# Four blocks in one first layer: a mixture of experts behind block attention on one core

## Chip, core and metric

The kernel runs on one core of a Trainium2 chip. The metric is device time in microseconds (us) of one launch, as the median of three runs.

## What is computed

The first part is a local-and-summary attention over 4 batches, 8 heads, 768 positions and 64 dimensions. Its output, 3072 rows of 512 numbers, is the input of the second part, a mixture of eight experts in which every row goes to one expert:

```python
logits = np.einsum('bsd,de->bse', x, w_gate)
local_gate = 1.0 / (1.0 + np.exp(-np.einsum('bsd,de->bse', x, w_local).squeeze(-1)))
...
            fresh_e = int(np.argmax(logits[b, s]))
            if s == 0 or local_gate[b, s] < 0.5:
                e = fresh_e
            else:
                e = prev_e if prev_e >= 0 else fresh_e
            prev_e = e
            ...
            h = np.maximum(x[b, s] @ w1[e], 0.0)
            out[b, s] = p[e] * (h @ w2[e])
```

All of it is fp32. The big products are made of three fp32r products each: both factors are split into a high and a low part, and high x high, high x low and low x high are added in PSUM.

## The kernel before, in words

**Attention** (lines 157 to 490) fills the first 120 us or so. While it runs, the rows of the first batch are routed, and the expert that most of them go to is chosen. Its two matrices are loaded and split, and blocks of 128 rows of that expert can start before the routing of the rest is known.

**Blocks and slots.** The rows of an expert are gathered in blocks of 128 by an indirect DMA on GpSimd (`gather`, L1027) into one of two buffers `xg`. `tx` (L1041) transposes a block on TensorE (four transposes, L1038) into a PSUM bank; ScalarE casts it to the high part (L1031) and VectorE subtracts for the low part (L1033), both into `xT`. `pair` (L1138) works on two blocks: its first layer has 8 slices of 128 hidden units, each 4 contraction steps of three matmuls with 256 columns (L1149 to L1151); every two slices share a PSUM bank, which ScalarE takes through ReLU (L1155) and VectorE finishes with the low part (L1157). Its second layer has for each block 8 steps of three matmuls with 512 columns (`mm`, L1055 to L1057), then `store` scales the rows and scatters them (L1081). `single` does one block.

**Order of the work.** All engines run their instructions in the order in which the program writes them. Blocks 0 to 5 are the early ones (`EARLY = 6`): three pairs of the first expert, whose instructions are interleaved with the steps of the routing by a small planner (`flow`, L543), which keeps estimated times of VectorE and TensorE and issues the next step of a chain (`self.steps`) when it thinks that it can run. `finish` is the chain of the second routing: some 65 small VectorE operations (L795 to L974) lead to a table of words, which two matmuls bring into one row (L978); the words say which expert each slot belongs to, and start the load of the next expert's two matrices into `stg`. Then 24 matmuls (L908) give the gather indices of blocks 6 and up, and after a softmax three products `bp` (L995) and 24 matmuls (L999) give `psort`, the rows' gate values.

**Placed steps.** During the second layer of a pair, at the step numbers in `PM`, `PM0`, `PW1` and `PW2`, the blocks of the next pair are transposed, and the matrices of the next expert are split, quarter by quarter: ScalarE casts 1024 columns (L1013), then VectorE (L1016) or GpSimd (L1021, four pieces) subtracts. A quarter of the second matrix can be cast only when the last block has used it. When a matrix is split, the load of a later one is started (`refill`). Blocks 6 to 13 are four sure pairs, with the steps of two experts that have fewer than 32 rows left (`few`) between; from 14 on a slot is a pair or a single by a test at run time. In this run two slots are singles, one of them the last.

Of the kernel before, what the change touches and what calls it, by code (L numbers as in the profile page):

```python
# [19 lines left out]
P = 128  # L20
NP = H // 2
# [26 lines left out]
FEW_AT = 34  # L48
# [16 lines left out]
PM, PM0 = (2, 5), (10, 13)  # L65
# [12 lines left out]
class Kernel:  # L78
# [962 lines left out]
    def tx(self, i, half=0, bank="t"):  # L1041

        ps = self.transposes(lambda c: self.xg[i % 2][:, c, G9:G9 + P], bank).rearrange("p (k t) -> p k t", k=KT)
        self.split_ps(ps, self.xT[:, :, 0, half], self.xT[:, :, 1, half])

    def th(self, src, name):
        ps = self.transposes(lambda c: src[:, P * c:P * c + P], "t")
        h, l = [self.fw.tile([P, 512], F32R, name=name + x) for x in "hl"]
        self.split_ps(ps, h, l)
        return h, l  # L1050
# [8 lines left out]
    def store(self, yp, i, act=False, alone=False):  # L1059
        while self.have_p <= i:  # L1060
            self.small(1, True)
        if i >= LATE and (i % 2 or alone):
# [3 lines left out]
        y = self.mw2.tile([P, 512], F32, name="yo", bufs=2)  # L1066
# [17 lines left out]
    def few_rows(self, j):  # L1084

        t = self.xm[j]
        self.nc.gpsimd.indirect_dma_start(out=t.rearrange("p a d -> p (a d)"), out_offset=None, in_=self.x_rows,
                                          in_offset=bass.IndirectOffsetOnAxis(ap=self.gidx[0:FEW, SLOTS + j:SLOTS + j + 1], axis=0))

    def few_prep(self, j):  # L1090

        nc, fw, b = self.nc, self.fw, j
        i = SLOTS + j
        ps = self.bank("t")
        for c in range(KT):
            nc.tensor.transpose(out=ps[:, FEW * c:FEW * c + FEW], in_=self.xm[b][:, c, G9:G9 + P], identity=self.ident[0:FEW, 0:FEW])
        nc.vector.tensor_copy(out=self.xf[b].rearrange("p k t -> p (k t)"), in_=ps[:, 0:KT * FEW])
        rp = fw.tile([FEW, 2], F32, name="rp")
        nc.vector.tensor_copy(out=rp[:, 0:1], in_=self.sidx[0:FEW, i:i + 1])
        nc.vector.tensor_copy(out=rp[:, 1:2], in_=self.psort[0:FEW, i:i + 1])  # L1100
        yield
        ps = self.bank("t")
        nc.tensor.matmul(out=ps[:, 0:2], lhsT=self.four, rhs=rp, start=True, stop=True)
        nc.vector.tensor_scalar(out=self.idx4[b], in0=ps[:, 0:1], scalar1=4.0, scalar2=self.c["quad"], op0=ALU.mult, op1=ALU.add)
        nc.vector.tensor_copy(out=self.p4[b], in_=ps[:, 1:2])

    def few(self, j):
# [12 lines left out]
        ps = self.bank("t")[:, 0:DF // 4]  # L1120
        for c in range(2):
            nc.tensor.transpose(out=ps[:, P * c:P * c + P], in_=h[:, P * c:P * c + P], identity=self.ident)
        hT = fw.tile([P, 2, 4, FEW], F32, name="fhT")
        nc.vector.tensor_copy(out=hT.rearrange("p c q t -> p (c q t)"), in_=ps)
        yield
        ps = self.bank("a")[:, 0:P]
        for f in range(FT):
            for q in range(4):
                c0 = f * DM + P * q
                nc.tensor.matmul(out=ps[FEW * q:FEW * q + FEW], lhsT=hT[:, f % 2, f // 2], rhs=s2[:, c0:c0 + P],  # L1130
                                 start=(f == 0), stop=(f == FT - 1))
        y = fw.tile([P, P], F32, name="fy")
        nc.vector.tensor_scalar(out=y, in0=ps, scalar1=self.p4[b], scalar2=None, op0=ALU.mult)
        nc.gpsimd.indirect_dma_start(out=self.out.rearrange("t (q d) -> (t q) d", q=4),
                                     out_offset=bass.IndirectOffsetOnAxis(ap=self.idx4[b], axis=0),
                                     in_=y, in_offset=None, bounds_check=4 * T_ALL - 1, oob_is_err=False)

    def pair(self, i, mid, w1, w2):  # L1138

        nc = self.nc  # L1140
        xT, hT = self.xT, self.hT
        for f in range(0, FT, 2):
            ps = self.bank("s").rearrange("p (f t) -> p f t", f=2)
            for j in range(2):
                for k in range(KT):
                    c0 = 2 * P * (KT * (f // 2) + k) + P * j
                    xh, xl = [xT[:, k, part].rearrange("p h t -> p (h t)") for part in range(2)]
                    wh, wl = [w[0][:, c0:c0 + P] for w in (self.hi, self.lo)]
                    nc.tensor.matmul(out=ps[:, j], lhsT=wh, rhs=xh, start=(k == 0), stop=False)  # L1149
                    nc.tensor.matmul(out=ps[:, j], lhsT=wh, rhs=xl, start=False, stop=False)  # L1150
                    nc.tensor.matmul(out=ps[:, j], lhsT=wl, rhs=xh, start=False, stop=(k == KT - 1))  # L1151
                    if k % 2:
                        yield
            h, l = hT[:, f:f + 2, 0], hT[:, f:f + 2, 1]
            nc.scalar.activation(out=h, in_=ps, func=AF.Relu)  # L1155
            self.dve(0.6, self.t + 0.5)
            nc.vector.scalar_tensor_tensor(out=l, in0=ps, scalar=0.0, in1=h.bitcast(F32), op0=ALU.max, op1=ALU.subtract)  # L1157
        for half in range(2):
            yp = self.ya if half and 2 * i >= LATE else self.bank("a")
            s = slice(P * half, P * half + P)  # L1160
            for f in range(FT):
                self.mm(yp, hT[:, f, 0, s], hT[:, f, 1, s], 1, lambda t: t[:, f * DM:f * DM + DM], f == 0, f == FT - 1)
                yield
                j = FT * half + f
                pm = PM if i else PM0
                if j in pm:
                    mid(pm.index(j))
                for at, w in (PW1, w1), (PW2, w2):
                    if j in at and j < 2 * FT - 1:
                        w(*(q for q in range(4) if at[q] == j))  # L1170
            self.store(yp, 2 * i + half, 2 * i < EARLY)
            if half:
                w2(*(q for q in range(4) if PW2[q] == 2 * FT - 1))
        yield

    def single(self, i, mid, w1, w2):

        nc, fw = self.nc, self.fw
        hs = [fw.tile([P, 512], F32, name=f"hs{f}") for f in range(2)]

        def mm1(f, ks):
            for k in ks:
                if k == 0:
                    self.hp = self.bank("s")
                self.mm(self.hp.rearrange("p (a c) -> p a c", a=2), self.xT[:, k, 0, 0], self.xT[:, k, 1, 0], 0,
# [6 lines left out]
        hT = [self.th(hs[0], "h0"), None]  # L1192
# [10 lines left out]
        hT[1] = self.th(hs[1], "h1")  # L1203
        mm2((2, 3))
        for h in range(2):
            mid(h)
        w1(2, 3)
        mm2(range(4, 8))
        self.store(yp, i, alone=True)
        w2(0, 1, 2, 3)  # L1210

    def run(self):
# [54 lines left out]
        def block0():  # L1267
# [3 lines left out]
            self.xT = self.mw2.tile([P, KT, 2, 2, P], F32R, name="xT")  # L1271
            self.hT = self.mw2.tile([P, FT, 2, 2 * P], F32R, name="hT")
# [269 lines left out]
```

## Time and profile before

| | us |
|---|---|
| median of 3 runs (426.94 to 427.31) | 427.31 |
| the profiled execution's own time | 427.81 |
| its span, first to last instruction | 425.9 |
| TensorE matmuls busy in the span | 407.5 |
| VectorE busy | 225.0 |
| ScalarE busy | 180.2 |
| GpSimd busy | 195.2 |

The span is what the rows lie in; 1.9 us of the profiled execution lie around it. A busy matmul row is longer than the distance to the next one, since matmuls are pipelined: how fast TensorE goes is read from the distance between starts. A row's line number is that of the kernel before; in a timeline the bracket says how long the engine stood idle before the row, and what ended that.

### The profile page before, as it was taken

The numbers are of one execution on the slowest core, as the hardware profiler recorded it, in microseconds if no ns is written. First come the engines' busy times: TensorE is split into PE (matmuls) and PEld (weight loads), VectorE is DVE, ScalarE is ACT, GpSimd is POOL, SyncE is SP. The second block draws the span as 40 slices with busy tenths as digits, with TensorE's granted clock in tenths as the row PEclk, the third lists the DMA queues.
The fourth block names the chain that finished last, engine by engine and source line by source line (L and its number), as shares of the span: only waits on it lengthen the run. The fifth ranks groups of instructions, "written<-read, shape, count | busy, mean of one in ns | idle before, by whom it ended". The sixth has DMA issues, their size and how long they took to land. (4 is left out here: it accounts for less than half of the span.)

```text
span 425.9 us, 11477 instructions
## 1 busy us (share of the span) xinstructions
PE 407.5 (96%) x4216; PEld 352.3 (83%) x4216; DVE 225.0 (53%) x478; ACT 180.2 (42%) x423; POOL 195.2 (46%) x290
## 2 busy tenths in 40 slices
PE   7889999999999999999999999999999999999992
PEld 6668777778798898989879889898987998989771
DVE  4678979989696785774222312217321822222620
ACT  3879877778872221164201101117312820211640
POOL 5398767776587401266511200207730752020570
PEclk9999999999999999999999999999999999999998
DMA  8999999999590303918787600201951483020010
GB/s 295 415 408 408 407 403 413 399 414 368 153 335 0 106 2 121 373 49 311 291 345 266 241 29 3 85 25 47 332 183 54 178 299 101 13 83 27 3 52 31
DMA packets 21956, 85.89 MB, mean 202 GB/s; under 512 B 2638, under 2 KB 3152, under 8 KB 18800
## 3 DMA queue, kind: packets, MB, share of 16 engines
q1 hardware_dynamic: 17600, 70.46, 43.3%
q0 software_dynamic: 4128, 14.22, 9.9%
q8 instruction: 40, 0.66, 0.6%
q14 instruction: 44, 0.36, 0.3%
q10 hardware_dynamic: 144, 0.20, 0.2%
HBM read 71.40 MB, written 13.60 MB: 200 GB/s over the span
## 5 line engine op out<-in xcount | busy, mean ns | idle before, releaser
L1149 PE MATMUL bs<-xT,h 128*128 128x256 f32 x352 | 100.5, 285 | 0.0
L1150 PE MATMUL bs<-xT,h 128*128 128x256 f32 x352 | 99.8, 283 | 0.0
L1151 PE MATMUL bs<-xT,l 128*128 128x256 f32 x352 | 99.5, 283 | 0.0
L1155 ACT ACTIVATE hT<-bs 128x512 fp32r<-128x512 f32 x44 | 26.3, 597 | 111.0 <-PE bs L1151 109.3
L1055 PE MATMUL ba<-h,hT 128*128 128x512 f32 x176 | 71.6, 407 | 0.3 <-PEq L1333 0.2
L1149 PEld LDWEIGHTS bs<-xT,h 128*128 128x128 f32 x352 | 67.4, 192 | 1.7 <-issue 1.2
L1057 PE MATMUL ba<-h,hT 128*128 128x512 f32 x176 | 68.8, 391 | 0.0
L1056 PE MATMUL ba<-l,hT 128*128 128x512 f32 x176 | 68.8, 391 | 0.0
L1157 DVE SCALAR_TENSOR_TENSOR hT<-bs,hT 128x512 fp32r<-128x512 f32 x44 | 30.4, 690 | 72.7 <-ACT hT L1155 53.1
L1150 PEld LDWEIGHTS bs<-xT,h 128*128 128x128 f32 x352 | 67.5, 192 | 0.8 <-issue 0.5
L1151 PEld LDWEIGHTS bs<-xT,l 128*128 128x128 f32 x352 | 67.5, 192 | 0.0
L1027 POOL DMA_INDIRECT xg<-x_dram,gidx x26 | 29.9, 1151 | 70.7 <-PE bt L1038 30.3
L1081 POOL DMA_INDIRECT out_dram<-yo,sidx x22 | 24.8, 1127 | 73.6 <-ACT yo L1068 27.3
L346 ACT ACTIVATE pr<-bs,nm 128x120 f32<-128x120 f32 x192 | 52.0, 381 | 5.0 <-DVE nm L342 4.9
L1021 POOL TENSOR_TENSOR l<-stg,h 128x256 fp32r<-128x256 f32 x48 | 42.0, 907 | 21.3 <-ACT h L1013 21.1
L1057 PEld LDWEIGHTS ba<-h,hT 128*128 128x128 f32 x176 | 33.0, 188 | 7.4
L1055 PEld LDWEIGHTS ba<-h,hT 128*128 128x128 f32 x176 | 33.1, 188 | 6.9 <-ACTq L1323 0.5
L1056 PEld LDWEIGHTS ba<-l,hT 128*128 128x128 f32 x176 | 33.2, 189 | 5.6
L280 POOL COPY vw<-gs 24x444 f32<-24x444 f32 (+1 forms) x56 | 29.3, 550 | 18.4 <-issue 13.7
L1013 ACT CAST h<-stg 128x1024 fp32r<-128x1024 f32 x32 | 32.7, 1053 | 6.5 <-PE ba L1057 5.4
L367 PE MATMUL ba<-vw,pt 121*64 121x74 f32 x768 | 32.1, 231 | 1.3 <-POOL vw L280 0.8
L1016 DVE TENSOR_TENSOR l<-stg,h 128x1024 fp32r<-128x1024 f32 x20 | 26.6, 1339 | 12.0 <-ACT h L1013 10.4
(276 smaller groups left out, 629.5 us busy)
## 6 DMA issues: line engine op xcount, KB each, us to landing
stg<-in_w SPq DMA_DIRECT2D x16, 1024.0 KB, 7.4
vw<-in_vW SPq DMA_DIRECT2D x16, 888.0 KB, 9.9
raw<-in_w SPq DMA_DIRECT2D x8, 1024.0 KB, 9.8
x_dram<-xs SPq DMA_DIRECT2D x8, 876.0 KB, 9.0
kp<-in_kT SPq DMA_DIRECT2D x16, 384.0 KB
q<-in_qT SPq DMA_DIRECT2D x16, 384.0 KB, 11.2
vt<-in_vT SPq DMA_DIRECT2D x16, 384.0 KB, 10.5
wst<-in_w SPq DMA_DIRECT2D x8, 512.0 KB, 8.0
```

Source lines behind the costliest of these rows:

```text
L346: nc.scalar.activation(out=pr[:, h, u, :], in_=sp[:, h, u, :], func=AF.Exp, bias=nm[:, h, u:u + 1], scale=1.0)
L367: nc.tensor.matmul(out=ap[64 * c:64 * c + 64, u, h, :], lhsT=pt[0:W + 1, h, u, 64 * c:64 * c + 64], rhs=vw[n % NVW][0:W + 1, 2 * (NG * g + ...
L1013: self.nc.scalar.copy(out=hi, in_=src)
L1021: eng.tensor_tensor(out=lo[:, p], in0=src[:, p], in1=hi[:, p].bitcast(F32), op=ALU.subtract)
L1027: self.nc.gpsimd.indirect_dma_start(out=t.rearrange("p a d -> p (a d)"), out_offset=None, in_=rows, in_offset=bass.IndirectOffsetOnAxis(ap ...
L1055: nc.tensor.matmul(out=ps, lhsT=ah, rhs=wh, start=first, stop=False)
L1056: nc.tensor.matmul(out=ps, lhsT=ah, rhs=wl, start=False, stop=False)
L1057: nc.tensor.matmul(out=ps, lhsT=al, rhs=wh, start=False, stop=last)
L1149: nc.tensor.matmul(out=ps[:, j], lhsT=wh, rhs=xh, start=(k == 0), stop=False)
L1150: nc.tensor.matmul(out=ps[:, j], lhsT=wh, rhs=xl, start=False, stop=False)
L1151: nc.tensor.matmul(out=ps[:, j], lhsT=wl, rhs=xh, start=False, stop=(k == KT - 1))
L1157: nc.vector.scalar_tensor_tensor(out=l, in0=ps, scalar=0.0, in1=h.bitcast(F32), op0=ALU.max, op1=ALU.subtract)
```

## The change

Blocks 2 to 5 become one slot: `quad` has a first layer of 8 slices with 512-column matmuls over the four blocks, one PSUM bank a slice, with ReLU and low part in two halves of 256 columns, then four second layers. All four blocks are transposed during the second layer of blocks 0 and 1 (`PM0`), blocks 6 to 9 during the quad's latter half (`PM4`), and from slot 6 on the blocks of the slot after the next. For that `xT` has four places, `xg` four buffers and `hT` a second tile. The two raw matrices of a few-row expert share one buffer, and their products stand elsewhere. The last output rows are scaled by VectorE alone. The core of the diff:

```diff
-FEW_AT = 34
+FEW_AT = ((1, 26, 29, 36, 40, 57), (37, 59, 62, 76, 80, 98))
...
-PM, PM0 = (2, 5), (10, 13)
+PM, PM0, PM4 = (2, 5), (3, 6, 11, 14), (18, 21, 24, 27)
...
+    def buffer(self, i):
+        return i if i < 2 else (i - 2) % 4
+
     def gather(self, i):
-        t = self.xg[i % 2]
+        t = self.xg[self.buffer(i)]
...
     def last_rows(self):
-        y, h = self.yl, slice(256, 512)
-        self.nc.vector.tensor_scalar(out=y[:, 0:256], in0=self.ya[:, 0:256], scalar1=self.pl, scalar2=None, op0=ALU.mult)
-        self.nc.scalar.activation(out=y[:, h], in_=self.ya[:, h], func=AF.Copy, scale=self.pl)
-        self.scatter(y, self.il)
+        self.nc.vector.tensor_scalar(out=self.yl, in0=self.ya, scalar1=self.pl, scalar2=None, op0=ALU.mult)
+        self.scatter(self.yl, self.il)
...
+    def second(self, i, blocks, mids, w1, w2):
+
+        for b in range(blocks):
+            late = i >= LATE and b == blocks - 1
+            yp = self.ya if late else self.bank("a")
+            s = slice(P * (b % 2), P * (b % 2) + P)
+            hT = self.hT[b // 2]
+            for f in range(FT):
+                self.mm(yp, hT[:, f, 0, s], hT[:, f, 1, s], 1, lambda t: t[:, f * DM:f * DM + DM], f == 0, f == FT - 1)
+                yield
+                j = FT * b + f
+                if j in mids:
+                    mids[j]()
+                k = j - FT * (blocks - 2)
+                for at, n, w in (PW1, k if i < EARLY else j, w1), (PW2, k, w2):
+                    if n in at and n < 2 * FT - 1:
+                        w(*(q for q in range(4) if at[q] == n))
+            self.store(yp, i + b, i < EARLY, late)
+        w2(*(q for q in range(4) if PW2[q] == 2 * FT - 1))
+        yield
+
+    def relu(self, ps, h, l):
+        self.nc.scalar.activation(out=h, in_=ps, func=AF.Relu)
+        self.dve(0.6 if len(h.shape) > 2 else 0.4, self.t + 0.5)
+        self.nc.vector.scalar_tensor_tensor(out=l, in0=ps, scalar=0.0, in1=h.bitcast(F32), op0=ALU.max, op1=ALU.subtract)
...
+    def quad(self, i, *calls):
+
+        nc = self.nc
+        xh, xl = [[self.xT[:, k, part].rearrange("p h t -> p (h t)") for k in range(KT)] for part in range(2)]
+        for f in range(FT):
+            ps = self.bank("s")
+            for k in range(KT):
+                c0 = 2 * P * (KT * (f // 2) + k) + P * (f % 2)
+                wh, wl = [w[0][:, c0:c0 + P] for w in (self.hi, self.lo)]
+                nc.tensor.matmul(out=ps, lhsT=wh, rhs=xh[k], start=(k == 0), stop=False)
+                nc.tensor.matmul(out=ps, lhsT=wh, rhs=xl[k], start=False, stop=False)
+                nc.tensor.matmul(out=ps, lhsT=wl, rhs=xh[k], start=False, stop=(k == KT - 1))
                 yield
...
+            for h in range(2):
+                self.relu(ps[:, 2 * P * h:2 * P * h + 2 * P], *(self.hT[h][:, f, part] for part in range(2)))
+        yield from self.second(i, 4, *calls)
...
-        first = chain(block0(), self.pair(0, *calls(2)))
+        first = chain(block0(), self.pair(0, *calls(2, dict(zip(PM0, range(2, 6))))))
...
-            rest = chain(first, *(self.pair(i, *calls(2 * i + 2)) for i in range(1, EARLY // 2)))
+            rest = chain(first, self.quad(2, *calls(6, dict(zip(PM4, range(6, 10))))))
             while self.steps:
                 next(rest, None)
                 self.flow(C_T)
```

Three places where the planner and the new code move instructions. In brackets stands which engine's semaphore an instruction waits for; a matmul of L1055 to L1057 has L1059 to L1061 in the changed kernel, the first layer of a pair L1180 to L1182, L1013 and L1016 keep their numbers.

TensorE, at the sorting matmuls L999. Before, within the second layer of blocks 4 and 5:

```order
L1055 MATMUL ba<-h_2480,hT 128x512 [waits Activation_49]
L1323 UNCONDITIONAL_BRANCH x2
L1056 MATMUL ba<-l_2482,hT 128x512
L1057 MATMUL ba<-h_2480,hT 128x512 [waits DVE_49]
L1055 MATMUL ba<-h_2480,hT 128x512
L1056 MATMUL ba<-l_2482,hT 128x512
L1057 MATMUL ba<-h_2480,hT 128x512
L999 LDWEIGHTS A
L999 MATMUL bt<-bp,A 128x120 [waits DVE_49]
```

Now, behind the last second-layer step of block 5 (L1353 ends a split's test):

```order
L1353 UNCONDITIONAL_BRANCH
L1060 MATMUL ba_3374<-l_2482,hT_2789 128x512
L1061 MATMUL ba_3374<-h_2480,hT_2789 128x512
L1059 MATMUL ba_3374<-h_2480,hT_2789 128x512
L1060 MATMUL ba_3374<-l_2482,hT_2789 128x512
L1061 MATMUL ba_3374<-h_2480,hT_2789 128x512
L1353 UNCONDITIONAL_BRANCH
L999 LDWEIGHTS A [waits DVE_49]
L999 MATMUL bt<-bp,A 128x120 [waits PE_49]
L999 LDWEIGHTS A
```

The 24 matmuls, which stood six steps into the second layer of blocks 4 and 5, now stand after all of it, ahead of the first layer of blocks 6 and 7.

VectorE, at the three sorting products L995. Before, ahead of the splits of the next expert's first matrix (L1016 into `l_2481`):

```order
L990 TENSOR_TENSOR eqp<-c_82,blk 128x960
L995 TENSOR_TENSOR bp<-eqp,p_87 128x24x40 [waits DVE_49]
L1157 SCALAR_TENSOR_TENSOR hT<-bs,hT 128x2x256 [waits Activation_49]
L995 TENSOR_TENSOR bp<-eqp,p_87 128x24x40
L1157 SCALAR_TENSOR_TENSOR hT<-bs,hT 128x2x256 [waits Activation_49]
L995 TENSOR_TENSOR bp<-eqp,p_87 128x24x40
L1294 TENSOR_LOAD words [waits DVE_49]
L1323 COMPARE_AND_BRANCH
L1016 TENSOR_TENSOR l_2481<-stg_2782,h_2479 128x1024 [waits DMAHW5_49,DMAHW2_49,Activation_49]
```

Now the third, behind the split of the third quarter of its second matrix (`l_2482`):

```order
L1016 TENSOR_TENSOR l_2482<-stg_2783,h_2480 128x1024 [waits DMAHW0_49,Activation_49]
L1353 UNCONDITIONAL_BRANCH
L1353 UNCONDITIONAL_BRANCH [waits DVE_49]
L1353 COMPARE_AND_BRANCH
L1328 UNCONDITIONAL_BRANCH
L1353 UNCONDITIONAL_BRANCH
L995 TENSOR_TENSOR bp<-eqp,p_87 128x24x40
L1417 UNCONDITIONAL_BRANCH
L1002 TENSOR_REDUCE psort<-bt 128x40 [waits PE_49]
```

The last product moved behind the five splits and four transposed blocks that VectorE does in the quad's latter half.

ScalarE, at the ReLU of blocks 2 to 5 (L1155, now L1165). Before, with the casts and outputs of blocks 0 and 1 ahead:

```order
L1155 ACTIVATE hT<-bs 128x2x256 [waits PE_49]
L1013 CAST h_2480<-wst_2544 128x1024 [waits DMAHW2_49]
L1155 ACTIVATE hT<-bs 128x2x256 [waits PE_49]
L1068 ACTIVATE yo<-ba,psort 128x512 [waits DVE_49,PE_49]
L1031 CAST xT<-bt 128x4x128 [waits PE_49,Activation_49] x2
L1068 ACTIVATE yo<-ba_2841,psort 128x512 [waits PE_49]
L1155 ACTIVATE hT<-bs 128x2x256 [waits DVE_49,PE_49] x4
L1031 CAST xT<-bt 128x4x128 [waits DVE_49,PE_49] x2
```

Now:

```order
L1165 ACTIVATE hT_2529<-bs 128x2x256 [waits PE_49]
L1034 CAST xT<-bt 128x4x128 [waits PE_49] x2
L1072 ACTIVATE yo<-ba,psort 128x512 [waits PE_49,DVE_49,Activation_49,Pool_49]
L1034 CAST xT<-bt 128x4x128 [waits PE_49] x2
L1072 ACTIVATE yo<-ba_2859,psort 128x512 [waits PE_49]
L1165 ACTIVATE hT_2529<-bs 128x256 [waits PE_49]
L1165 ACTIVATE hT_2789<-bs 128x256 [waits DVE_49]
L1165 ACTIVATE hT_2529<-bs 128x256 [waits PE_49]
```

One activation over 512 columns became two over 256, and the second of them waits for VectorE.

## Rows read from the trace of the kernel before

**Rows 1.** Stretches: us, span, busy PE, PEld, DVE, ACT, POOL (count), PEclk, DMA share, GB/s.
```profile
200.00:410.00 210.00, 209.20 (x1454) 184.61 (x1454) 68.89 (x100) 55.87 (x79) 72.30 (x75) 1.00 0.38 136
418.00:422.00 4.00, 0.20 (x1) 0.00 (x0) 0.48 (x1) 0.47 (x1) 0.98 (x1) 1.00 0.19 72
422.00:425.90 3.90, 0.00 (x0) 0.00 (x0) 0.00 (x0) 0.00 (x0) 0.00 (x0) 0.50 0.00 0
```

**Rows 2.** Timeline, PE: start us, us, form; first-layer matmuls, then second-layer ones.
```profile
145.45 0.28 PE L1149 MATMUL bs<-xT,h 128*128 128x256 f32 x1
...
156.48 0.28 PE L1151 MATMUL bs<-xT,l 128*128 128x256 f32 x1
...
161.85 0.39 PE L1056 MATMUL ba<-l,hT 128*128 128x512 f32 x1
...
164.14 0.39 PE L1057 MATMUL ba<-h,hT 128*128 128x512 f32 x1
```

**Rows 3.** Timeline, blocks 2, 3: last transpose to their first layer.
```profile
143.06 0.60 PE L1038 MATMUL bt<-ident,xg 128*128 128x128 f32 x4
...
144.37 0.69 DVE L1033 TENSOR_TENSOR xT<-bt,xT 128x512 fp32r<-128x512 f32 x1 [0.96 <-ACT xT L1031]
...
144.88 0.28 PE L1149 MATMUL bs<-xT,h 128*128 128x256 f32 x1
...
145.11 0.38 PE L1150 MATMUL bs<-xT,h 128*128 128x256 f32 x1
```

**Rows 4.** Timeline, first and last VectorE step before the table of words, and PE.
```profile
144.97 0.16 DVE L795 TENSOR_TENSOR nbi<-cnt,adj 128x8 int32<-128x8 f32 x1
...
163.23 0.16 DVE L974 TENSOR_TENSOR w<-w,cend 128x1 f32<-128x1 f32 x1
...
164.46 0.32 PE L978 MATMUL bt<-ident,w 128*1 128x46 f32 x4
```

**Rows 5.** Groups, VectorE, 145.1 to 163.4: what stood between those steps.
```profile
L1157 DVE SCALAR_TENSOR_TENSOR hT<-bs,hT 128x512 fp32r<-128x512 f32 x4 | 2.7, 687 | 1.3 <-ACT hT L1155 1.3
L1033 DVE TENSOR_TENSOR xT<-bt,xT 128x512 fp32r<-128x512 f32 x2 | 1.4, 692 | 1.4 <-ACT xT L1031 1.4
```

**Rows 6.** Groups by shape, all stretches: ReLU, its remainder, and a scaled copy.
```profile
L1155 ACT ACTIVATE hT<-bs 128x512 fp32r<-128x512 f32 x44 | 26.3, 597 | 111.0 <-PE bs L1151 109.3 <-issue 1.7
...
L1157 DVE SCALAR_TENSOR_TENSOR hT<-bs,hT 128x512 fp32r<-128x512 f32 x44 | 30.4, 690 | 72.7 <-ACT hT L1155 53.1 <-ACTq L1323 13.1 <-issue 5.6
...
L1071 DVE TENSOR_SCALAR yo<-ba,psort 128x512 f32<-128x512 f32 x16 | 12.0, 749 | 25.0 <-PE ba L1057 23.2 <-issue 1.8
```

**Rows 7.** Timeline, the last output rows of the run: their two halves.
```profile
418.30 0.48 DVE L1076 TENSOR_SCALAR yl<-ba,pl 128x256 f32<-128x256 f32 x1 [2.77 <-PE ba L1057]
...
418.87 0.47 ACT L1077 ACTIVATE yl<-ba,pl 128x256 f32<-128x256 f32 x1 [4.18 <-DVE yl L1076]
```

**Rows 8.** Timeline, gather of block 6: its indices on VectorE, its issue on GpSimd.
```profile
171.62 0.20 DVE L774 COPY tl<-bt 128x40 f32<-128x40 f32 x1 [3.23 <-PE bt L908]
...
173.06 0.98 POOL L1027 DMA_INDIRECT xg<-x_dram,gidx  x1 [1.90 <-PE bs L1151]
```

**Rows 9.** The tile xg, all gathers.
```profile
DMA to landing us min/median/max: 5.4/7.6/8.1
```

**Rows 10.** The tile bp: the sorting products and the matmuls that read them.
```profile
L999 PE MATMUL bt<-bp,A x24: 216/216/226, 186.0 to 187.2; 128*128 128x120 bf16 x24
L995 DVE TENSOR_TENSOR bp<-eqp,p x3: 1147/1149/1159, 179.2 to 182.9; 128x960 bf16<-128x960 f32 x3
```

**Rows 11.** Timeline, end of block 5 and start of block 6.
```profile
193.44 1.05 ACT L1013 CAST h<-stg 128x1024 fp32r<-128x1024 f32 x1 [0.31 <-PE ba L1057]
...
194.52 1.28 DVE L1016 TENSOR_TENSOR l<-stg,h 128x1024 fp32r<-128x1024 f32 x1 [1.30 <-ACT h L1013]
194.56 0.28 PE L1149 MATMUL bs<-xT,h 128*128 128x256 f32 x1
```

**Rows 12.** The page, DMA issues: KB each and median us to landing.
```profile
raw<-in_w SPq DMA_DIRECT2D x8, 1024.0 KB, 9.8
```

More of the change, by code (lines that the diff above doesn't have):

```diff
@@ L1039, in transposes, with tx, th @@
         return ps
[L1041 to L1046, printed above, removed]
+    def tx(self, i, bank="t"):
+        ps = self.transposes(lambda c: self.xg[self.buffer(i)][:, c, G9:G9 + P], bank).rearrange("p (k t) -> p k t", k=KT)
+        at = (i - 2) % 4
+        self.split_ps(ps, self.xT[:, :, 0, at], self.xT[:, :, 1, at])
+    def th(self, src, i):
         ps = self.transposes(lambda c: src[:, P * c:P * c + P], "t")
-        h, l = [self.fw.tile([P, 512], F32R, name=name + x) for x in "hl"]
+        h, l = [self.hT[0][:, 2 * i + x].rearrange("p x t -> p (x t)") for x in range(2)]
         self.split_ps(ps, h, l)
@@ L1181, in mm1, with single @@
+    def single(self, i, mids, w1, w2):
+        nc = self.nc
+        at = (i - 2) % 4
+        hs = [self.lw.tile([P, 512], F32, name=f"hs{f}") for f in range(2)]
         def mm1(f, ks):
@@ L1202, in single @@
         mm2((0, 1))
-        hT[1] = self.th(hs[1], "h1")
+        hT[1] = self.th(hs[1], 1)
         mm2((2, 3))
-        for h in range(2):
-            mid(h)
+        for j in sorted(mids):
+            mids[j]()
         w1(2, 3)
         mm2(range(4, 8))
-        self.store(yp, i, alone=True)
+        self.store(yp, i, late=i >= LATE)
         w2(0, 1, 2, 3)
@@ L1406, in run, with few @@
             some = [reg(SLOTS + j, mybir.ALL_ENGINES, 1) for j in range(FEWS)]
+            def few(j, part):
+                with tc.If(some[j] > 0):
+                    part(j)
+                    if part == self.few_1:
+                        few_load(j, 1)
+                    elif part == self.few_3 and j + 1 < FEWS:
+                        few_load(j + 1, 0)
             steps = {}
             for j in range(FEWS):
-                n = FEW_AT * j
-                steps[n + 1] = lambda j=j: self.few_rows(j)
@@ L1411, in run @@
-                steps[n + 26], steps[n + 29] = [lambda g=g: next(g, None) for g in [self.few_prep(j)] * 2]
-                part = few_part(some[j], self.few(j))
-                for k in range(3):
-                    steps[n + FEW_AT + 2 + 4 * k] = part
-            steps[FEW_AT + 12] = lambda: few_load(1)
-            for i in range(EARLY // 2, PAIRS):
-                for n, _ in enumerate(self.pair(i, *calls(2 * i + 2))):
-                    steps.pop(n + FEW_AT * (i - EARLY // 2), int)()
@@ new lines, in slots, with slot @@
+            def slots(i0, i1, n=0):
+                for i in range(i0, i1, 2):
+                    c = i, i + 2, dict(zip(PM, (i + 4, i + 5)))
+                    if i < 2 * PAIRS:
+                        n = run(self.pair(i, *calls(*c[1:])), n)
+                    else:
+                        slot(*c)
+            def slot(i, *c):
+                two = reg(i + 1, mybir.ALL_ENGINES, 1)
+                kept = dict(st)
+                with tc.If(two > 0) as full:
+                    for _ in self.pair(i, *calls(*c)):
+                        pass
+                st.update(kept)
+                with full.Else():
+                    self.single(i, *calls(*c))
@@ L1426, in slots, with ends @@
+            nc.vector.memset(self.ya, 0.0)
+            def ends(i1, sure, more):
                 with ExitStack() as c:
-                    for i in range(i0, i1, 2):
-                        n = i + 2 if i + 2 < most else SLOTS
+                    for i in range(LATE, i1, 2):
                         if i >= sure:
```

200 lines of the change are left out of this document (88 added, 112 removed).

## The prediction

> **What bounds the kernel now.** I read first how busy each engine is by stretch. From 200 to 410 us TensorE is busy 209.2 of 210 us at the full clock, VectorE 68.9 [rows 1]: the end is set by TensorE alone, and whatever TensorE waits for or saves moves the end by as much. So the question is what the change does to the list of matmuls, and where that list meets an engine that isn't ready. Then the timeline of TensorE, for the distance between starts. In the first layer of blocks 2 and 3, 92 distances lie between 145.45 and 156.48: 0.120 us each for 256 columns. In a second layer ten lie between 161.85 and 164.14: 0.229 us for 512 columns [rows 2]. Then the timelines around the three places where the order changes.
>
> **The sum**, against the profiled execution (427.81 us); the median of the runs is 0.50 lower, and I forecast the median.
>
> 1. *The wider first layer.* Removed are 2 x 96 matmuls of 256 columns, 192 x 0.120 = 23.0 us; added 96 of 512 columns, 96 x 0.229 = 22.0. That is **-1.0 us**, all on the path (-0.9 to -1.2 for 2 ns either way). A wide matmul costs nearly two narrow ones, so the change's main part has little to give. The Trainium skill's TensorE: Matmul & The Clock Gate (Wait — 56ns, not 53.3ns?) gives a back-to-back distance of columns / 2.4 GHz plus about 2.5 ns, an estimate of 109 and 216 ns here; by it the gain were 0.25 us. The rows have 120 and 229, so the measurement decides.
>
> 2. *Rows that arrive late at the quad.* Each transposed block takes 0.45 us of TensorE (143.06 to 144.88 less six matmuls) [rows 3]. Their number stays, but two more now stand ahead of the second first layer, whose nominal start goes from 144.88 to 145.78. Before, the last transpose stood six matmuls ahead, and its low part ended at 145.06, 2.0 us after the transpose began; the second matmul, which reads it, started at 145.11, 0.11 late [rows 3]. Now three matmuls stand between: the transpose begins at 144.64, the low part is there at 146.69, and the second matmul was due at 146.01. Loss 0.68 less 0.11: **+0.6 us** (0.3 to 0.8). Blocks 4 and 5 are gathered into new buffers, so their gathers go out as soon as GpSimd's pieces of the split are done, well ahead.
>
> 3. *The table of words.* TensorE passes L978 at step 87 of the quad's first layer, 87 x 0.229 = 19.9 us in; it waits for VectorE's L974. Before, L795 began at 144.97 and L974 ended at 163.39, a full 1.07 us ahead of L978 at 164.46 [rows 4]. In these 18.4 us stood 4.1 us of first-layer and transposing work and 2.7 of waiting for ScalarE [rows 5], so the chain itself takes 11.6 (12.0 with overlapping ends). In the change six slices of the quad come before L974, and each is now two halves that take turns: ScalarE's second half waits for VectorE's first (the order shows the wait). ScalarE's copy of the last output's second half also began only when VectorE's had ended, 418.87 after 418.78 [rows 7]. A half on VectorE: 0.69 less the 0.27 by which a scaled copy of 256 columns (0.48) is shorter than one of 512 (0.75) is 0.42 [rows 6, 7]; a half ReLU lies between 0.30 (half of 0.60) and 0.47, I take 0.38. VectorE is held by a slice for 0.42 + 0.10 + 0.38 + 0.05 + 0.42 = 1.37 us. Chain 12.0, six slices 8.2, a first wait 0.6 and 0.2 for the last transposed block: L974 ends 21.0 into the first layer, 1.1 us after L978's turn. **+1.1 us** (0 to 2.2). Queued behind L974 on VectorE are the table's copy and the products that L908 reads; behind the table's copy, on SyncE, the loads of the next expert, needed only when the quad's last two blocks begin. So all of that is late by about as much as TensorE itself.
>
> 4. *The gather of block 6.* Before, gather 6 went out 1.4 us after VectorE took up its indices [rows 8], with most of a first layer still ahead of block 6's transposes. Now its indices' matmuls L908 stand 21 matmuls into the quad's second layers and block 6's transposes 57 in: 36 x 0.229 = 8.2 us between, of which about 1.4 goes to issue, so 6.8 are left; a gather lands 5.4 to 8.1 us after issue, 7.6 in the median [rows 9]. Late by -1.4 to 1.3; I take **+0.5** (0 to 1.3), below the median's 0.8 because no output stands ahead of it in GpSimd's queue now. Gathers 7 to 9 follow at about 1 us each on GpSimd [rows 8] and are used 2.5 us apart or more (nine matmuls and a transpose), so they come in time when the first does; the outputs of blocks 2 and 3 go behind them, and nobody waits for these.
>
> 5. *The sorting matmuls L999.* They cost 1.2 us in either place. Before they ran at 186.0, inside the second layer, with their third product begun at 182.9 [rows 10]. Now they stand between block 5's last matmul and block 6's first layer, and the third product stands behind VectorE's split of the second matrix's third quarter. That split can't be early: its cast waited for TensorE's use of the quarter (0.31, from PE), began at 193.44, and the split ran 194.52 to 195.80, while block 6's first layer began at 194.56 [rows 11]. With TensorE's end of block 5 as zero the split ends at 1.24; the product adds 1.15 and the signal 0.05. TensorE stands still **2.4 us**, and everything behind L999 with it; the two loads of words by TensorE's sequencer, formerly under running matmuls, may show behind it (no row here: 0 to 0.6), I take **+2.5** (2.1 to 3.2).
>
> 6. *The last output.* Two halves in turn, 418.30 to 419.34 [rows 7], become one VectorE operation of 0.75 [rows 6]: **-0.3 us**.
>
> At nothing: transposing two slots ahead (TensorE waited for no gathered row in those slots, and the number of transposes stays); a few-row expert's matrices in one buffer (the second is loaded after the first product and needed 21 steps of 0.7 us later, 15 us against 9.8 for a load [rows 12]; if two loads in turn took over 15 us, TensorE would wait for the rest); the ReLU's extra fixed costs on ScalarE, which is busy 56 of 210 us.
>
> Sum: -1.0 + 0.6 + 1.1 + 0.5 + 2.5 - 0.3 = +3.4, so 431.2 for the profiled execution and **430.7** for the median.
>
> **The rivals.**
> - *The two readers don't take turns* (12 in 100). If ScalarE's wait for VectorE is met early, a slice holds VectorE for 0.8, L974 is ready near 17.6, and term 3 is nothing: 429.6. Against it: the order and rows 7, though there both halves also wrote one tile. The Trainium skill's PSUM — Partial Sum Buffer (PSUM bank collisions raise a hardware error) says that two engines may not even read one bank at once; that speaks for turns, and no row here separates bank from tile.
> - *Faster: VectorE keeps ahead* (7 in 100). One place decides, the third product: if it ends before block 5's last matmul, L999 waits for nothing. VectorE would also have to be ahead at L974 and gather 6 in time, which a shorter chain would give together. Then -1.0 + 0.4 - 0.3 = -0.9, 426.4. Against it stands the order of both queues, and the cast that waits for TensorE.
> - *The waits are longer* (13 in 100): gather 6 lands at 8.1 us behind the later loads (+0.8), L974 is at its upper bound (+1.1), and the loads of words show (+0.5): 433.1. The clock is no part of it by itself: after the last matmuls (TensorE is busy only to 418.2) it was still full to 422.0 and half after that [rows 1], and a stand of 2.4 us is shorter than these 3.8.
> - *By the skill's distance between matmuls* (2 in 100) term 1 would be -0.25, and the time 431.5.
>
> **How the numbers follow.** The forecast, both waits about as priced, has 66 in 100: 430.7, between 429.6 and 432.1. A measurement of this kernel tells 0.2%, 0.9 us, from no change. The range of 8 in 10 leaves out the faster case, and some of the longest: 428.6 to 432.8. Faster by more than 0.2% is most of the second rival, 0.06; within 0.2% (426.5 to 428.2) the rest of it and the readers' case with a short L999, 0.09; slower 0.85.
>
> **What would show it.** In the changed profile: the quad's matmuls 0.229 apart; its second matmul started by VectorE's last transposed part; L978 idle about 1 us before it, released by VectorE; L999 idle about 2.4 us, released by the product; ScalarE's ReLU waiting for VectorE's at every second half; one scaled copy at the end. It would be wrong if TensorE passes L999 with no idle time, if matmuls of 512 columns over `xT` are not 0.229 apart, or if TensorE waits in slots 6 to 21, where I priced nothing.

## The result, and the profile after

| | before | the change |
|---|---|---|
| median, us | 427.12 (426.90 to 427.31, 4 runs) | 429.94 (429.48 to 430.72, 4 runs) |
| ratio to before | | 1.0068, interval 1.0051 to 1.0086 |
| span of the profiled execution | 425.9 | 428.3 |
| the first expert's first matmul starts at | 119.75 | 119.11 |
| the last matmul starts at | 417.80 | 420.55 |
| from the one to the other | 298.05 | 301.44 |

The change is slower by 2.8 us; 3.4 had been forecast for it. Most of the program ahead of the first expert is the same in both, and that part alone came out 0.64 us apart. So the accounts below begin at the first expert's first matmul: the change takes 3.39 us more from there to the last matmul, and 0.36 less behind it, 3.03 together.

The place where it is lost is the border between block 5 and block 6. The timeline of TensorE of the change, from block 5's last matmuls to block 6's first ones (start us, us, the instruction, and in the bracket the idle time before it and what ended it):

```profile
193.12 0.39 PE L1060 MATMUL ba<-l,hT 128*128 128x512 f32 x1
193.35 0.40 PE L1061 MATMUL ba<-h,hT 128*128 128x512 f32 x1
195.85 2.58 PE L999 MATMUL bt<-bp,A 128*128 128x120 bf16 x24 [2.10 <-DVE bp L995]
198.19 0.56 PE L1180 MATMUL bs<-xT,h 128*128 128x256 f32 x1
198.56 0.41 PE L1181 MATMUL bs<-xT,h 128*128 128x256 f32 x1
198.77 0.41 PE L1182 MATMUL bs<-xT,l 128*128 128x256 f32 x1
198.98 0.38 PE L1180 MATMUL bs<-xT,h 128*128 128x256 f32 x1
199.19 0.28 PE L1181 MATMUL bs<-xT,h 128*128 128x256 f32 x1
```

TensorE's last matmul of block 5 starts at 193.35, its next instruction is L999 at 195.85: 2.27 us more than the 0.23 of a distance. Then the 24 sorting matmuls take 2.34 us to the next start, where they took 1.27 before (185.99 to 187.26 there), and the first four distances of block 6 are 0.37, 0.21, 0.21 and 0.21 instead of 0.12. The tile `bp` says that TensorE waited 2.1 us for L995, and that each L999 took 308 ns against 216 [rows 10]:

```profile
L999 PE MATMUL bt<-bp,A x24: 282/308/308, 195.8 to 198.1; 128*128 128x120 bf16 x24
L995 DVE TENSOR_TENSOR bp<-eqp,p x3: 1148/1151/1157, 179.9 to 194.6; 128x960 bf16<-128x960 f32 x3
...
  DVE bp L995: 2.1, 1
```

The timeline of VectorE around it shows the queue order: the split of the second matrix's third quarter (L1016) waits 1.20 for ScalarE's cast, and the third product (L995) follows only behind it, at 194.64, as [rows 11] let one expect. That cast began at 192.42, right behind another cast; TensorE's last use of the quarter had ended only 0.07 earlier, so ScalarE could hardly have begun sooner.

```profile
184.59 1.15 DVE L995 TENSOR_TENSOR bp<-eqp,p 128x960 bf16<-128x960 f32 x1
...
193.50 1.23 DVE L1016 TENSOR_TENSOR l<-stg,h 128x1024 fp32r<-128x1024 f32 x1 [1.20 <-ACT h L1013]
194.64 1.15 DVE L995 TENSOR_TENSOR bp<-eqp,p 128x960 bf16<-128x960 f32 x1
```

The same stretch by windows (columns as in [rows 1]; the one with 1.00, 0.89, 0.50 is the granted clock) shows what the forecast had left out:

```profile
193.00:194.00 1.00, 0.75 (x4) 0.27 (x2) 0.50 (x1) 0.63 (x2) 0.84 (x2) 1.00 0.00 0
194.00:195.00 1.00, 0.00 (x0) 0.00 (x0) 1.00 (x2) 1.00 (x2) 1.00 (x1) 1.00 0.68 106
195.00:196.00 1.00, 0.15 (x2) 0.16 (x3) 0.79 (x1) 0.46 (x1) 0.69 (x2) 0.89 0.64 205
196.00:197.00 1.00, 1.00 (x12) 1.00 (x11) 0.00 (x0) 0.00 (x0) 0.90 (x1) 0.50 1.06 451
...
198.00:199.00 1.00, 1.00 (x9) 1.00 (x7) 0.40 (x2) 0.00 (x0) 0.69 (x2) 0.50 0.99 410
199.00:200.00 1.00, 1.00 (x9) 1.00 (x9) 0.00 (x0) 0.00 (x0) 0.97 (x2) 0.90 1.00 375
```

TensorE ends at 193.75 and stands; within the stretch from 195 to 196, about 2 us later (a mean of 0.89 puts it at 195.8), the granted clock goes from its full level (2.4 GHz) to half of it (1.2 GHz) and comes back only in the stretch from 199 to 200. L999 and the head of block 6 run at half clock.

The other three places. At the quad's start, TensorE's timeline (answers to [rows 2, 3]):

```profile
143.97 0.60 PE L1041 MATMUL bt<-ident,xg 128*128 128x128 f32 x4
...
145.25 0.50 PE L1197 MATMUL bs<-xT,h 128*128 128x512 f32 x1
145.97 0.50 PE L1198 MATMUL bs<-xT,h 128*128 128x512 f32 x1 [0.23 <-DVE xT L1036]
146.31 0.39 PE L1199 MATMUL bs<-xT,l 128*128 128x512 f32 x1
...
165.37 0.39 PE L1199 MATMUL bs<-xT,l 128*128 128x512 f32 x1
165.69 0.32 PE L978 MATMUL bt<-ident,w 128*1 128x46 f32 x4
```

The second matmul (L1198) starts 0.72 after the first where 0.23 would do: 0.49 lost, from VectorE's last low part (L1036, 145.23 to 145.92). From 146.31 to 165.37 there are 84 distances of 0.227 us. L978, priced to wait 1.1 us, starts 0.32 after the matmul ahead of it, just as it did before (164.14 to 164.46, [rows 2, 4]): nothing lost. VectorE's steps behind these (answers to [rows 4, 5]):

```profile
145.23 0.69 DVE L1036 TENSOR_TENSOR xT<-bt,xT 128x512 fp32r<-128x512 f32 x1 [0.96 <-ACT xT L1034]
145.84 0.15 DVE L795 TENSOR_TENSOR nbi<-cnt,adj 128x8 int32<-128x8 f32 x1
...
158.34 0.42 DVE L1167 SCALAR_TENSOR_TENSOR hT<-bs,hT 128x256 fp32r<-128x256 f32 x1
159.21 0.43 DVE L1167 SCALAR_TENSOR_TENSOR hT<-bs,hT 128x256 fp32r<-128x256 f32 x1 [0.45 <-ACT hT L1165]
...
165.42 0.16 DVE L974 TENSOR_TENSOR w<-w,cend 128x1 f32<-128x1 f32 x1
```

L974 ends at 165.58, 0.11 ahead of L978; 158.34 and 159.21 are the two halves of one slice, with ScalarE's second half between them. At block 6's transposes TensorE waits for the gather (answers to [rows 8]), 0.53 more than a distance:

```profile
181.91 0.40 PE L1061 MATMUL ba<-h,hT 128*128 128x512 f32 x1
182.67 0.66 PE L1041 MATMUL bt<-ident,xg 128*128 128x128 f32 x4 [0.37 <-DMA xg<-x_dram,gidx]
```

And at the end one scaled copy stands where two halves did [rows 7]. From the last matmul's start to the scatter it was 1.82 us before (417.80 to 419.62) and is 1.46 now. The scatter before, then the end of the change:

```profile
419.62 0.98 POOL L1081 DMA_INDIRECT out_dram<-yl,il  x1 [6.78 <-ACT yl L1077]
```

```profile
420.55 0.39 PE L1061 MATMUL ba<-h,hT 128*128 128x512 f32 x1
420.98 0.75 DVE L1079 TENSOR_SCALAR yl<-ba,pl 128x512 f32<-128x512 f32 x1 [2.64 <-PE ba L1061]
422.01 0.99 POOL L1083 DMA_INDIRECT out_dram<-yl,il  x1 [6.52 <-DVE yl L1079]
```

### The profile page after: what moved, and what is told of

Same layout as the page of the kernel before. It is cut to its first block, busy times and chain, and to the rows that moved or that the text cites. A ratio compares the mean times of both kernels' runs of the same rounds, so it can differ in the third digit from the quotient of the medians.

```text
span 428.3 us, 11331 instructions
## 1 busy us (share of the span) xinstructions
PE 408.3 (95%) x4120; PEld 348.2 (81%) x4120; DVE 225.7 (53%) x486; ACT 180.5 (42%) x429; POOL 193.6 (45%) x290
## 5 line engine op out<-in xcount | busy, mean ns | idle before, releaser
L1180 PE MATMUL bs<-xT,h 128*128 128x256 f32 x288 | 82.6, 287 | 0.0
L1165 ACT ACTIVATE hT<-bs 128x512 fp32r<-128x512 f32 (+1 forms) x52 | 27.7, 532 | 129.0 <-PE bs L1182 109.3
L1181 PE MATMUL bs<-xT,h 128*128 128x256 f32 x288 | 81.7, 284 | 0.0
L1182 PE MATMUL bs<-xT,l 128*128 128x256 f32 x288 | 81.6, 283 | 0.0
L1059 PE MATMUL ba<-h,hT 128*128 128x512 f32 x192 | 78.1, 407 | 0.3
L1061 PE MATMUL ba<-h,hT 128*128 128x512 f32 x192 | 75.2, 392 | 0.0
L1060 PE MATMUL ba<-l,hT 128*128 128x512 f32 x192 | 75.0, 391 | 0.0
L1167 DVE SCALAR_TENSOR_TENSOR hT<-bs,hT 128x512 fp32r<-128x512 f32 (+1 forms) x52 | 31.6, 608 | 77.3 <-ACT hT L1165 67.6
L1180 PEld LDWEIGHTS bs<-xT,h 128*128 128x128 f32 x288 | 55.5, 193 | 1.4 <-issue 1.0
L1181 PEld LDWEIGHTS bs<-xT,h 128*128 128x128 f32 x288 | 55.5, 193 | 0.5 <-issue 0.2
L1182 PEld LDWEIGHTS bs<-xT,l 128*128 128x128 f32 x288 | 55.3, 192 | 0.0
L1061 PEld LDWEIGHTS ba<-h,hT 128*128 128x128 f32 x192 | 36.0, 188 | 8.2
L1059 PEld LDWEIGHTS ba<-h,hT 128*128 128x128 f32 x192 | 36.1, 188 | 7.6 <-issue 0.7
L1013 ACT CAST h<-stg 128x1024 fp32r<-128x1024 f32 x32 | 32.4, 1050 | 6.3 <-PE ba L1061 2.9
L367 PEld LDWEIGHTS ba<-vw,pt 121*64 121x64 f32 x768 | 27.2, 136 | 6.5 <-issue 3.8
```

What stands on the lines that cost most here:

```text
L367: nc.tensor.matmul(out=ap[64 * c:64 * c + 64, u, h, :], lhsT=pt[0:W + 1, h, u, 64 * c:64 * c + 64], rhs=vw[n % NVW][0:W + 1, 2 * (NG * g + ...
L1013: self.nc.scalar.copy(out=hi, in_=src)
L1059: nc.tensor.matmul(out=ps, lhsT=ah, rhs=wh, start=first, stop=False)
L1060: nc.tensor.matmul(out=ps, lhsT=ah, rhs=wl, start=False, stop=False)
L1061: nc.tensor.matmul(out=ps, lhsT=al, rhs=wh, start=False, stop=last)
L1167: self.nc.vector.scalar_tensor_tensor(out=l, in0=ps, scalar=0.0, in1=h.bitcast(F32), op0=ALU.max, op1=ALU.subtract)
```

## The experiments

All ratios are to the kernel before, from runs on the same chip. It took 427.65 us beside the first four kernels below the change and 427.60 beside the last three, so their ratios are not quotients with the 427.12 of the first row. The column "path" is the time from the first expert's first matmul to the last matmul of each kernel's profiled execution.

| kernel | median, us | ratio (interval) | path, us |
|---|---|---|---|
| before | 427.12 | | 298.05 |
| the change | 429.94 | 1.0068 (1.0051 to 1.0086) | 301.44 |
| products together | 426.65 | 0.9979 (0.9968 to 0.9989) | 297.87 |
| TensorE kept busy | 429.32 | 1.0035 (1.0024 to 1.0045) | 299.97 |
| one split on GpSimd | 427.84 | 0.9998 (0.9989 to 1.0008) | 298.50 |
| before, last rows by VectorE | 427.42 | 0.9991 (0.9981 to 1.0000) | 298.93 |
| block 5 turned earlier | 425.39 | 0.9946 (0.9932 to 0.9959) | 296.76 |
| halves reordered | 425.51 | 0.9945 (0.9931 to 0.9959) | 296.77 |
| block 6 turned later | 424.99 | 0.9933 (0.9919 to 0.9946) | 296.37 |

**The three products together.** In `finish`, the planner gets the three products of `bp` as one step, so they all stand ahead of the first split on VectorE's queue, and L999 goes into block 5's second layer:

```diff
-        for i in range(3):
-            yield "LONG"
+        yield "LONG"
+        for i in range(3):
+            self.dve(C_LONG if i else 0.0)
             v.tensor_tensor(out=bp[:, :, i, :], in0=eq, in1=self.p3[:, :, i, :].to_broadcast([P, NT, n]), op=ALU.mult)
```

> The change with the three sorting products issued together, ahead of every split of the next expert, so that the sorting matmuls L999 stand in block 5's second layer. Theory A (the stand at L999 and the half clock behind it are the whole loss; 2.27 us of standing, 1.07 more for L999 itself and 0.52 more in block 6's first layer, 3.86 together): about 426.1 us, ratio to the kernel before 0.998, L999 at 216 ns with no wait, block 6's first matmul some 0.23 us after block 5's last. Theory B (the stand only hid a later lateness, of the splits or of the transposed rows of blocks 6 and 7): the wait moves to block 6's first layer, and the time stays within 1 us of 429.9, ratio above 1.004.

Measured: 426.65, ratio 0.9979; path 3.57 us shorter than the change's, of 3.86 expected. The tile `bp` now:

```profile
L999 PE MATMUL bt<-bp,A x24: 216/216/226, 184.0 to 185.2; 128*128 128x120 bf16 x24
L995 DVE TENSOR_TENSOR bp<-eqp,p x3: 1145/1160/1206, 179.9 to 182.1; 128x960 bf16<-128x960 f32 x3
```

The matmuls are back at 216 ns with no wait for a product, and block 6 follows block 5 by 0.23 us (194.79 to 195.02). Theory A holds, B falls: nothing was hidden behind the stand. Without it the change is faster than before.

**TensorE kept busy through the wait.** Ten matmuls of 512 columns into a free bank stand right ahead of L999, and nobody reads their result:

```diff
-        m = self.bank("t")
+        w, m = self.bank("t"), self.bank("t"); [nc.tensor.matmul(out=w, lhsT=self.A[:, t, :], rhs=..., ...) for t in range(10)]
```

> The change with ten matmuls of 512 columns on a free PSUM bank right ahead of L999, whose result nobody reads; TensorE then works for 2.2 us where it stood. Theory A1 (the clock fell because TensorE stood): the granted clock stays 1.00, L999 takes 216 ns, the time falls by 1.6 us to about 428.3, ratio 1.003. Theory A2 (the clock fell for another cause, the loads of the next words, the form of L999, or the run): L999 stays at about 308 ns and the time at 429.9 or up to 0.3 above, ratio 1.007.

Measured: ratio 1.0035, path 1.47 us shorter than the change's. TensorE's timeline at the place (nine of the ten appear in it):

```profile
194.01 0.40 PE L1061 MATMUL ba<-h,hT 128*128 128x512 f32 x1
194.25 2.33 PE L997 MATMUL bt<-A 128*128 128x512 bf16 x9
196.51 1.43 PE L999 MATMUL bt<-bp,A 128*128 128x120 bf16 x24
197.81 0.36 PE L1180 MATMUL bs<-xT,h 128*128 128x256 f32 x1
198.01 0.28 PE L1181 MATMUL bs<-xT,h 128*128 128x256 f32 x1
```

L999 still comes 2.5 us behind block 5's last matmul, for the product is as late as ever. But its 24 matmuls take 1.30 us to the next start, and block 6 goes on at 0.12 from its second matmul on. The granted clock is 1.00 in every stretch from 193 to 200. Its mean over a whole run agrees with that: 0.992 to 0.997 in the ten runs of this kernel, 0.991 to 0.993 in the four of the change. So of the loss at this place about 1.5 us is the clock and the rest the wait, and the clock fell because TensorE stood: A1 holds.

**One split on GpSimd.** L999 stays behind block 5's last matmul; only the split ahead of the third product leaves VectorE's queue:

```diff
-                eng = nc.vector if SPLIT_BY[w][q] == "V" else nc.gpsimd
+                eng = nc.vector if SPLIT_BY[w][q] == "V" and (self.have_p == COLS or (w, q) != (1, 2)) else nc.gpsimd
```

> The change with one split, that of the second matrix's third quarter inside the quad, on GpSimd instead of VectorE; L999 stays where the change has it, behind block 5's last matmul, and the third product is still issued last. Theory A (it is VectorE's queue, the split ahead of the third product, that makes TensorE stand): the product runs from about 192.3 to 193.5, L999 waits under 0.2 us, the clock stays, about 426.2 us, ratio 0.998. Theory C (it is the place of L999 at the border of two slots, with two loads of words behind it): TensorE still stands over 1 us there, ratio above 1.003.

Measured: ratio 0.9998, path 2.94 us shorter than the change's, of 3.7 expected. The clock stays full, so the queue was the cause and C falls; but L999 still comes 0.40 late, since the product took 1.70 us instead of 1.15. GpSimd was then busy with four pieces of an earlier split (the moved split ran there only from 203 us on). The third piece began just ahead of the product and took its usual time; the fourth took 1.64 us instead of the 0.74 of the same piece in the change. VectorE's timeline, then GpSimd's:

```profile
193.10 1.70 DVE L995 TENSOR_TENSOR bp<-eqp,p 128x960 bf16<-128x960 f32 x1
```

```profile
193.05 0.73 POOL L1021 TENSOR_TENSOR l<-stg,h 128x256 fp32r<-128x256 f32 x1
193.75 1.64 POOL L1021 TENSOR_TENSOR l<-stg,h 128x256 fp32r<-128x256 f32 x1
```

The Trainium skill's SBUF — State Buffer (SBUF: two separate sides) says that VectorE and GpSimd share one pair of ports, and that between a VectorE instruction with two SBUF inputs and a GpSimd one that reads SBUF, whoever holds it makes the other wait for the whole instruction. The trace agrees: the product is longer by about what was left of the third piece (0.55 and 0.68 us), and the fourth piece ends 0.59 after the product; no run here shows the port itself. Another 0.46 went at the first few-row expert, whose 32 matmuls took 2.32 us to the next start instead of 1.86; the tile `raw` puts 0.3 of it to the load:

```profile
  PEld bs L1117: 0.3, 1
```

**The kernel before, with the last rows by VectorE alone.** The edit is the change's, made to the kernel before:

```diff
-        self.nc.vector.tensor_scalar(out=y[:, 0:256], ...)
-        self.nc.scalar.activation(out=y[:, h], in_=self.ya[:, h], ...)
+        self.nc.vector.tensor_scalar(out=y, in0=self.ya, scalar1=self.pl, ...)
```

> The kernel before with the last output rows in one VectorE operation instead of two halves. Theory A (the halves take turns, so one operation ends sooner): from the last matmul's start to the scatter 1.46 us instead of 1.82, the time 0.36 lower, 426.8, ratio 0.999 (within the noise of the times; the trace tells). Theory D (the halves overlap): the scatter goes out no sooner, 427.1 to 427.3. The start of the first expert's first matmul, 119.75 before and 119.11 in the change, shows here whether those 0.64 us belong to the change: 119.7 if they do.

Measured: ratio 0.9991, by its interval not told from no change, and 1.46 us from the last matmul's start (417.67) to the scatter (419.13), as theory A says. The first expert's first matmul starts at 118.74 here, and in the other profiles between 119.11 and 120.03: that start varies by over a microsecond from one execution to another, and the 0.64 us were no part of the change. The path is 0.88 longer than before; 0.67 of that lies where a pair hands over to a block alone (322.04 there, 321.04 here, one start each, with 0.59 and 1.26 us to the next). Nothing in the edit is near it.

**Block 5 turned one step earlier.** On top of the products together:

```diff
-PM, PM0, PM4 = (2, 5), (3, 6, 11, 14), (18, 21, 24, 27)
+PM, PM0, PM4 = (2, 5), (3, 6, 11, 13), (18, 21, 24, 27)
```

> The kernel with the three products together, and the transpose of block 5 one step earlier (four matmul groups of the second layer behind it would be five matmuls more; here six matmuls stand behind it instead of three). Theory A (the quad's second matmul waits for block 5's low part, and VectorE's way to L974 is paced from the quad's first slice on, so it moves along): the distance of the first two matmuls falls from 0.72 to about 0.3, L974 and L978's turn both come 0.45 sooner, the wait of L978 stays near 0.1, time 0.45 under the kernel with the products together, ratio 0.997. Theory B (the chain before L974 doesn't move): L978 waits 0.5, and the time is that of the kernel with the products together, ratio 0.998.

Measured: ratio 0.9946, path 1.11 us shorter than with the products together. The quad's head and L978:

```profile
145.43 0.40 PE L1197 MATMUL bs<-xT,h 128*128 128x512 f32 x1
145.67 0.44 PE L1198 MATMUL bs<-xT,h 128*128 128x512 f32 x1
```

```profile
165.32 0.32 PE L978 MATMUL bt<-ident,w 128*1 128x46 f32 x4
```

The second matmul follows by 0.24, and L978 comes 19.89 us after the quad's start (20.46 with the products alone, 145.29 to 165.75). So L974 and L978's turn moved together, as A says, and 0.57 of the gain is this. The rest is 0.25 less waiting for block 6's gather (0.34 instead of 0.59), 0.11 in blocks 0 and 1, and 0.11 where a pair hands over to a block alone; why these moved isn't settled, and each is of the size that such places vary by.

**The halves reordered.** On top of that, ScalarE's two halves of a slice stand first, then VectorE's two:

```diff
-            for h in range(2):
-                self.relu(ps[...], *(self.hT[h][:, f, part] for part in range(2)))
+                [nc.scalar.activation(out=g(h)[:, 0], in_=s(h), func=AF.Relu) for h in range(2)]; [(..., nc.vector.scalar_tensor_tensor(out=g(h)[:, 1], in0=s(h), ...)) for h in range(2)]
```

> The same, and in the quad ScalarE's two half ReLUs issued first, then VectorE's two remainders, so that the two engines take turns once per slice instead of twice. Theory A (turns on one PSUM bank hold VectorE for 1.29 us a slice): a slice holds it for about 0.85, L974 ends some 2.5 us ahead of L978, L978 waits for nothing; TensorE gains 0.1 at most, ratio as for the kernel with block 5's transpose earlier, 0.997. Theory B (VectorE is held by its own fixed costs, not by turns): a slice still takes 1.2 us or more, and L974 ends where it did.

Measured: ratio 0.9945, path as before the edit. One slice on VectorE, and L974:

```profile
157.36 0.76 DVE L1202 SCALAR_TENSOR_TENSOR hT<-bs,hT 128x256 fp32r<-128x256 f32 x2
...
163.77 0.16 DVE L974 TENSOR_TENSOR w<-w,cend 128x1 f32<-128x1 f32 x1
```

Both halves take 0.76 us, against 1.29 where the engines took turns twice (158.34 to 159.63 above). L974 is 1.5 us ahead of L978 (163.93 and 165.40), not 2.5, because VectorE now waits for ScalarE's part of a slice. That the turns held VectorE is shown; that they cost TensorE nothing, too. Whether they come from the shared bank or from the program's order of waits, no run here tells.

**Block 6 turned one step later.** On top of that, with the planner told of the products' time before it places L999, which puts it behind block 5 again:

```diff
-PM, PM0, PM4 = (2, 5), (3, 6, 11, 13), (18, 21, 24, 27)
+PM, PM0, PM4 = (2, 5), (3, 6, 11, 13), (19, 22, 25, 28)
...
-        yield "PE"
+        yield 0.1; yield "PE"
```

> The same, with block 6's transposes one step later (19 instead of 18, the next three at 22, 25 and 28) and L999 issued once the third product's time in the planner's books is up, which puts it behind block 5's last matmul again, now with the product long done. Theory A (TensorE waits 0.4 to 0.5 for the gather of block 6, and L999's place costs nothing when its product is there): no wait at block 6's transposes, none at L999, granted clock 1.00, time 0.45 under the kernel before in this list, about 425.7, ratio 0.996. Theory B (the border of the slots costs by itself, or the next transposes come late): TensorE waits 0.3 us or more at block 6's first layer or at later transposes, ratio 0.997 or above.

Measured: 424.99, ratio 0.9933, path 0.40 us shorter. L999 has the change's late place and its product was done at 182.55:

```profile
192.13 0.39 PE L1061 MATMUL ba<-h,hT 128*128 128x512 f32 x1
192.36 1.43 PE L999 MATMUL bt<-bp,A 128*128 128x120 bf16 x24
193.67 0.35 PE L1180 MATMUL bs<-xT,h 128*128 128x256 f32 x1
```

It starts one distance behind block 5 and takes 1.31 us; the granted clock is 1.00 from 188 to 200. Theory A holds: the place costs nothing, the late product did. This version is faster than both kernels, by 0.67% than the one before.

## Why the prediction was right, and where it wasn't

The sign and the size were right (+3.4 forecast, +2.8 measured, 429.94 within 428.6 to 432.8), and so was the place of the largest term. Two terms were wrong by more than a microsecond each, with opposite signs (+1.4 and -1.1). That the sum came so near is luck: the two nearly cancel, and +3.03 in the profiled executions stands against the +3.4.

| term | forecast | measured | from |
|---|---|---|---|
| 1, wider first layer | -1.0 | -1.2 | 96 x 0.227 against 23.0 |
| 2, rows late at the quad | +0.6 | +0.4 | 0.49 less 0.11 [rows 3] |
| 3, table of words | +1.1 | 0.0 | L978 at 0.32, as before |
| 4, gather of block 6 | +0.5 | +0.5 | 0.76 less 0.23 |
| 5, sorting matmuls | +2.5 | +3.9 | 2.27 + 1.07 + 0.52 |
| 6, last output | -0.3 | -0.4 | 1.46 against 1.82 |

The 0.52 is block 6's first layer, 12.03 us against 11.51. The sum is +3.2, and 3.03 were measured. Two places outside the table moved as well, by +0.57 and -0.82 (behind the list); with them the sum is +3.0.

- **Term 5, the step that failed** is the sentence that the clock "is no part of it by itself". The stand was priced right, by the right cause (2.27 us; shown by the kernels with the products together and with the split on GpSimd), and the two loads of words behind it cost nothing (1.31 us from L999 to block 6 in the last kernel, 1.27 for L999 before). But the forecast took 3.8 us at the end of the run, after which the clock was still full, as a bound for a stand of 2.4. That was one instance, and the change shows another: down about 2 us after TensorE stopped. Keeping TensorE busy through the same wait gave 1.5 us back.
- **Term 3, the step that failed** is L978's turn at 19.9 us into the first layer. Term 2's wait lies inside that layer, so it moves the turn as well: 0.49 was counted twice. L978 came 20.44 us after the layer's start. And L974 ended 20.33 after it, not 21.0: a slice held VectorE for 1.29 us, not 1.37, six times, and the rest of the chain had been taken 0.2 too long. Turns there were, so the rival without them falls, though its time, 429.6, was the nearest; they just didn't decide. The margin was narrow: L974 ended 0.11 us ahead of L978.
- **Terms 1, 2, 4 and 6** stand as priced. A wide matmul costs 0.227 us, where the rows had 0.229. The estimate of 0.216 from the Trainium skill's TensorE: Matmul & The Clock Gate (Wait — 56ns, not 53.3ns?) isn't what this trace shows.
- **What was costed at nothing** came out near nothing only in sum. TensorE waits for no gathered row but block 6's, and for no load of a few-row expert. But it loses time in one place and saves it in another, as the rows behind this list show.
- **The faster rival** named the place that decides, the third product. Where that is early, the change is 0.2% faster than before, as that rival's 426.4 said; the number agrees better than the sum behind it, for block 6's gather still cost 0.59 us there.

The place where time is lost: the second product of the first few-row expert takes 2.46 us in the change (244.16 to 246.62) where it took 1.89 (229.34 to 231.23). The profile names no engine that TensorE waited for. All seven kernels with the quad have this, at 2.44 to 2.50. It is one of the prediction's own signs of being wrong, a wait in slots 6 to 21, and its cause is open. The end of that product in the change:

```profile
246.05 0.64 PE L1136 MATMUL bs<-raw,fhT 128*32 128x128 f32 x11 [0.17 <-issue]
```

The place where time is saved: where a pair hands over to a block alone, two matmuls lay 0.59 and 0.69 us apart before (from 322.04 and from 405.33), and the change has 0.23 twice. The forecast counted nothing there. The two kernels without the quad lose 0.8 and 1.6 us at these places together, the seven with it at most 0.2; which part of the change does it, no run here tells. The first of them, before:

```profile
322.04 0.39 PE L1057 MATMUL ba<-h,hT 128*128 128x512 f32 x1
322.63 0.48 PE L1055 MATMUL bs<-h,xT 128*128 128x512 f32 x1 [0.20 <-PE ba L1057]
```

## What to carry to other kernels

A stand of the bounding engine is not only its own length: when TensorE stopped for 2.3 us at full clock, 1.6 more went at half clock behind it, so price both, and take no single stretch that stayed at full clock for a bound. Waits on one engine lie one behind the other, so an earlier wait must be taken off the later ones. And where a planner runs out of work to interleave, look at what is left at its end: here one product of 1.15 us, queued behind a split whose cast can't start before TensorE has used the old matrix, turned a change that gains 0.2% into one that loses 0.7%.

## What the hardware showed that was not expected

- The granted clock fell about 2 us after TensorE stopped at 193.75, and after the last matmul of the same execution (ended 420.94) only in the stretch from 424 to 425, 3.5 us later. TensorE was as busy in the 10 us before the one as before the other. Over the nine profiled executions the time from the last matmul's end to the fall lies between 3.0 and 5.3 us. So the 3.8 us that the forecast used were one draw out of a spread; what sets it, no run here tells.
- Ahead of their last matmuls, and once the clock was full, the nine executions have two stands of TensorE longer than 1.6 us. One is the change's; the other is in attention, in the kernel with the halves reordered: 2.07 us, from 7.83 to 9.90. There too the granted clock went to half, in the stretch from 11 to 12, when TensorE had been back at work for over a microsecond; it came back in the stretch from 14 to 15. None of the shorter stands is followed by half clock. Two instances are not a rule.
- VectorE's product of 128x960 took 1.70 us beside GpSimd's pieces of a split and 1.15 in the change, and a piece of 128x256 beside the product 1.64 instead of 0.74.
- The start of the first expert varied between 118.74 and 120.03 us over nine profiled executions with nearly the same work ahead of it, more than most of the terms above.
